# Summing the convolution taps of the first two blocks in PSUM with transposes, and taking the first unit's weights first

## The chip, the cores and the metric

One core of a Trainium2 chip runs the whole program. The metric is the device time of one execution in microseconds, lower is better; a run's number is the median of several executions. Beside it stands one execution taken with the hardware profiler, whose span reaches from its first to its last instruction.

The engines by the names that the profile uses: PE is TensorE's matmul and PEld its weight load, DVE is VectorE, ACT is ScalarE, POOL is GpSimd, and SP is SyncE, which issues all of this kernel's DMAs.

## The reference

Three steps follow each other. x has the shape (2, 4096, 192) and the generated weights (2, 4096, 8, 7).

```python
w = softmax(weight_gen over its last axis)          # 7 taps for each of 8 heads
x_unf = x_pad[:, s + k, :]                          # k = 0..6, six zeros ahead
out[b, s, h, g] = sum_k w[b, s, h, k] * x_unf[b, s, k, h, g]   # 24 channels a head
x = out.reshape(8192, 192)
g = max(0.01 * (x @ w_in), x @ w_in)                # 192 -> 2048
x = g @ w_out                                       # 2048 -> 192
h = x @ w2_in
g = where(h > 0, h, exp(min(h, 0)) - 1)
x = g @ w2_out
```

All of it is fp32.

## The kernel before, in words

**Tiles.** The 8192 tokens are cut into 16 blocks of 512: 128 partitions with 4 consecutive tokens each (BS = 4). A block passes through a convolution, layer 0 and layer 1. Each layer has 2048 hidden channels, worked in 8 units of 256.

**Two parts for every operand.** To keep fp32 exactness at the PE's faster fp32r rate, every activation and every weight is split into a high part, rounded to fp32r, and a low part, the rest. A product takes three matmuls: low by high, high by low, high by high. Activations are split by ACT (the rounded copy) and DVE (the subtraction).

**Weights** (`split`, lines 196 to 259) come from memory as raw 8-byte words. SP loads a piece into a buffer of the ring `raw` (three buffers); ACT takes the fraction (L217) and the exponent part (L221) into a buffer of ring `t` (two); DVE joins bits (L228, L231) and adds (L238); ACT writes the high part (L241), DVE the low one (L246). `split_in` (lines 264 to 269) makes pieces of the in-weights, `part` 0 for input channels 0 to 127 and `part` 1 for the other 64, folded; `split_out` makes pieces of the out-weights. The first unit of layer 0 needs a piece of 256 columns and one of 128.

**Convolution** (`conv_block`, lines 281 to 411). SP loads the block's generated weights (L288, 112 KB) and its x with six tokens ahead (L291, 960 KB). DVE and ACT make the softmax (L298 to L311). Then DVE multiplies tap by tap (L331), the first tap into the tile `a`, the others into `prod`, and adds each `prod` to `a` (L339): 7 multiplies and 6 adds, each 768 elements a partition. ACT copies channels 128 to 191 doubled side by side (`double`, L374). The PE transposes: 16 matmuls with an identity, each 64 partitions by 128 columns onto 64 output columns, 8 from the doubled copy and 8 from `a` (L388), into the PSUM bank that later holds the block's sums of layer 0. ACT and DVE split the result into `yt` or `xt` (`high`, L393, `low`, L396), the input of layer 0.

**Units.** `phases` (line 182) gives the order of blocks and layers. Blocks 0 and 1 of layer 0 run interleaved, one unit of one, one unit of the other, so that a piece of weights lasts for two units; then block 2 of layer 0, blocks 0 and 1 of layer 1, and from there one phase of each layer in turn. The first four units (`LAG = 4`) have only their in-matmuls (`whole`, line 699: six over the whole array, six over halves of its rows, two at a time), from then on a round (`both`, line 712) interleaves one unit's in-matmuls with the out-matmuls of the unit four before. A unit's tile `h` in PSUM (two buffers) is read by ACT (L552, leaky, or L555 and L559 for layer 1), which makes the high part too (L569); DVE makes the low one (L572).

**The order of the work.** Nothing is ordered by the engines: `Plan.order` (lines 78 to 127) simulates the five queues at build time with estimated costs, and the program is issued in the order that it finds. Whenever an engine is free, it takes the ready task with the smallest key among those whose buffers are free in the rings; a unit's matmuls have the key `s`, its number, and a task gives its buffers back when all its users have ended. For a convolution block with due date `due`, multiplies and adds have keys from `due - 0.8` backwards in steps of `2 * PACE`; block 0 is due at -13.5, block 1 at -0.5. Weight pieces have keys around the number of the unit that needs them first, for the first two 0: load at -6, bits at -1.6, low at -0.7. On the chip each engine works its queue in that order and waits on semaphores.

```python
a = plan.add({"q": max(0.45, 1.44 * z)}, key - 6, load, takes=[raw], delay=2.3)
f = plan.add({"a": 0.2 + 0.46 * z}, key - 1.9, fraction, [a], uses=[raw])
b = plan.add({"a": 0.2 + 0.46 * z}, key - 1.9, unbias, [a], [t], [raw])
b = plan.add({"d": 0.29 + 0.8 * z}, key - 1.6, bits, [b], uses=[t, raw])
b = plan.add({"d": 0.15 + 0.53 * z}, key - 1.3, add, [b, f], uses=[raw, t])
```

Of the kernel before, what the change touches and what calls it, by code (L numbers as in the profile page):

```python
# [8 lines left out]
F32 = mybir.dt.float32  # L9
F32R = mybir.dt.float32r  # L10
I32 = mybir.dt.int32
U32 = mybir.dt.uint32
I64 = mybir.dt.int64
AF = mybir.ActivationFunctionType
ALU = mybir.AluOpType
AX = mybir.AxisListType

P = 128
D = 192
DFF = 2048  # L20
H = 8
K = 7
G = D // H
# [3 lines left out]
BS = 4  # L27
NB = SP // BS
N = BS * P
# [8 lines left out]
AHEAD = 1  # L38

PACE = 0.28  # L40


class Task:
# [87 lines left out]
def conv_moe_kernel(ctx: ExitStack, tc: tile.TileContext, x, wg, wi0, wi1, wo, out):  # L131
    nc = tc.nc

    rings = {
        "xs": (2, [P, BS + PAD, D], F32), "ws": (2, [P, BS * H, K], F32),
        "st": (1, [P, BS * H, 3], F32), "a": (1, [P, BS, D], F32), "prod": (1, [P, BS * D], F32),
        "xt": (1, [P, 4, N], F32R), "yt": (2, [P, 4, N], F32R),
        "h": (2, [P, 2, N], F32), "w": (3, [P, 2 * N], F32),
        "gh": (4, [P, 2 * N], F32R), "gl": (4, [P, 2 * N], F32R),
        "c": (1, [P, N], F32), "o": (1, [P, N], F32),  # L140
        "raw": (3, [P, 512], I64), "t": (2, [P, 512], I32),
    }
    const = ctx.enter_context(tc.tile_pool(name="const", bufs=1))
    sb = ctx.enter_context(tc.tile_pool(name="sb", bufs=1))
# [4 lines left out]
    plan = Plan({r: bufs for r, (bufs, _, _) in rings.items()})  # L149
# [3 lines left out]
    def new(slot):  # L153
        bufs, shape, dt = rings[slot.ring]
        if bufs == 1 or slot.ring == "h":

            tiles, n = lasting.setdefault(slot.ring, ([], [0]))
            if len(tiles) < bufs:
                pool = {"h": ps, "st": small}.get(slot.ring, sb)
                tiles.append(pool.tile(shape, dt, name=f"{slot.ring}{len(tiles)}"))  # L160
            slot.tile = tiles[n[0] % bufs]
            n[0] += 1
            return slot.tile
        pool = small if slot.ring == "ws" else sb
        slot.tile = pool.tile(shape, dt, tag=slot.ring, name=slot.ring, bufs=bufs)
        return slot.tile

    ident = const.tile([P, P], F32, name="ident")
    spare = const.tile([P, 1], F32, name="spare")
    win = {}  # L170
# [15 lines left out]
    bank = {p: acc[n % 2] for n, p in enumerate(phases)}  # L186
# [74 lines left out]
    def first(l, u):  # L261
        return min(at[l, i, u] for i in range(2))

    def split_in(l, part, m0, m1):
        c = slice(m0 // 2 * P, m1 // 2 * P) if part else slice(m0 * P, m1 * P)
        lo = [(win[l, part, 1][:, c], slice(None))]
        names = [("in", l, u) for u in range(m0 // 2, m1 // 2)]
        src = (wi0, wi1)[part][l][:, c]
        split(src, win[l, part, 0][:, c], lo, first(l, m0 // 2), names)

    def split_out(l, k0):
        w = wout[l][:, k0 : k0 + 2, :]
# [5 lines left out]
    xts = {}  # L278
    stored = {}

    def conv_block(i, due):

        xs, ws, st, a = Slot("xs"), Slot("ws"), Slot("st"), Slot("a")
# [29 lines left out]
        first = due - 0.8 - 2 * K * PACE  # L313
        lw = plan.add({"q": 0.45}, first - 8, load_w, takes=[ws], delay=2.3)
        lx = plan.add({"q": 2.7}, first - 7.9, load_x, takes=[xs], delay=2.3)
        t = plan.add({"d": 0.68}, first - 3, top, [lw], [st], [ws])
        t = plan.add({"a": 0.3}, first - 2, exp, [t], uses=[ws])
        t = plan.add({"d": 0.75}, first - 1, total, [t], uses=[ws, st])
        t = plan.add({"d": 0.35}, first - 0.5, scale, [t], uses=[ws, st])
        prod = Slot("prod")  # L320
# [18 lines left out]
            nc.vector.tensor_tensor(out=sums(), in0=sums(), in1=prods(), op=ALU.add)  # L339

        y = [t, lx]
        for k in range(K):
            key = due - 0.8 - PACE * 2 * (K - 1 - k)
            takes = [[a], [prod]][k] if k < 2 else []
            uses = [r for r in [xs, ws, a] + [prod] * (k > 0) if r not in takes]
            y = [plan.add({"d": 0.95}, key, lambda k=k: mult(k), y, takes, uses)]
            if k:
                y = [plan.add({"d": 0.95}, key, add, y, uses=[a, prod])]
        last = y

        x_t = Slot("yt" if i < 2 else "xt")
        xts[0, i] = x_t

        place = Slot("h") if i == 2 else None

        def at_place():
            return place.tile if place else bank[0, i]

        def parts(j):

            return at_place()[:, :, j * N // 2 : (j + 1) * N // 2]

        def slot(j):
            return x_t.tile[:, j, :].rearrange("p (a b) -> p a b", a=2)

        twice = Slot("o")

# [19 lines left out]
                        c = (j * BS + s) * 64  # L387
                        nc.tensor.transpose(at_place()[:, half, c : c + 64], src, ident[r, r])  # L388

        def high(j):  # L390
            if not j:
                new(x_t)
            return nc.scalar.activation(slot(2 * j), parts(j), AF.Copy).ins  # L393

        def low(j):
            return nc.vector.tensor_tensor(  # L396
                out=slot(2 * j + 1), in0=parts(j), in1=slot(2 * j).bitcast(F32), op=ALU.subtract
            ).ins

        n = phases.index((0, i))  # L400
        free = stored[phases[n - 2]] if i > 2 else []
        p = [place] if place else []
        t = plan.add({"a": 0.6}, due - 0.2, double, last + free, [twice], [a])
        t = plan.add({"pe": 0.95}, due, transpose, [t], p, [a, twice])

        k = due + (0.3 if i < 3 else 1.35)
        b = plan.add({"a": 0.55}, k, lambda: high(0), [t], [x_t], p)
        c = plan.add({"a": 0.55}, k + 0.1, lambda: high(1), [b], uses=[x_t] + p)
        b = plan.add({"d": 0.66}, k + 0.2, lambda: low(0), [b], uses=[x_t] + p)
        c = plan.add({"d": 0.66}, k + 0.3, lambda: low(1), [c], uses=[x_t] + p)  # L410
        return [b, c]

    def evac(l, i, after, key):
        A, B = (bank[l, i][:, j, :] for j in range(2))
# [240 lines left out]
    low = {}  # L655
# [130 lines left out]
```

## Time and profile before

| | |
|---|---|
| median of 3 runs | 1167.04 us (1166.29 to 1167.16) |
| the profiled execution | 1164.52 us |
| its span | 1162.7 us |
| PE busy | 1119.4 us, 96% |
| DVE busy | 808.2 us, 70% |
| ACT busy | 788.3 us, 68% |
| multiplies of the convolution into `prod` (L331) | 96, 955 ns each |
| its adds (L339) | 96, 955 ns each |

The busy time of an engine is the sum over its instructions; its share is of the span. The matmuls overlap in a pipeline, so a busy PE need not be at its peak. The profile is of one execution, 2.5 us faster than the median of the runs.

### The profile page before, as it was taken

The page shows a single profiled execution, that of the slowest core. Times are in us where ns is not written, and L with a number is a line of the kernel's source. Part 1 is how long each engine was busy: PE and PEld are TensorE (multiplying, and loading weights), DVE is VectorE, ACT ScalarE, POOL GpSimd, SP SyncE. Part 2 cuts the span into 40 slices and gives each one's busy share as a digit, 9 for nine tenths or more (in the row PEclk, how much of TensorE's full clock was granted, in tenths as well). Part 3 has the DMA queues.
Part 4 walks back from the last instruction along what each step waited for, and adds up shares of the span by engine and source line. Part 5 has one row for each costly group of instructions (what it writes and reads, how often), then busy time and mean ns, then how long its engine had stood idle before and what let it go on. Part 6 is the DMA issues. An engine that isn't in the chain of part 4 may idle for free.

```text
span 1162.7 us, 23771 instructions
## 1 busy us (share of the span) xinstructions
PE 1119.4 (96%) x9920; PEld 930.9 (80%) x9920; DVE 808.2 (70%) x1050; ACT 788.3 (68%) x1022; POOL 0.7 (0%) x6
## 2 busy tenths in 40 slices
PE   0699999999999999999999999999999999999998
PEld 0488998888888888888888888888888888888886
DVE  8999998948568494865948578494865839464464
ACT  1687898658586675857658576675857657585675
POOL 0000000000000000000000000000000000000000
PEclk9999999999999999999999999999999999999999
DMA  3424230000101001010100101001010000000000
GB/s 136 147 87 127 76 94 15 19 35 2 52 1 52 2 1 52 1 53 2 52 1 1 53 1 52 1 1 53 1 53 1 15 1 1 15 2 15 1 1 28
DMA packets 12620, 37.97 MB, mean 33 GB/s; under 512 B 1504, under 2 KB 3680, under 8 KB 12512
## 3 DMA queue, kind: packets, MB, share of 16 engines
q1 hardware_dynamic: 12512, 36.44, 9.8%
q8 instruction: 78, 1.28, 0.5%
q14 instruction: 30, 0.25, 0.1%
HBM read 30.15 MB, written 6.29 MB: 31 GB/s over the span
## 4 chain that ended last, share of the span: by engine, by line
PE 96%; DVE 3%; DMA 0%; ACT 0%; issue 0%; ACTq 0%; SPq 0%; DVEq 0%
PE acc L630 50%; PE h L630 45%; DVE prod L331 1%; DVE a L339 1%; PE acc L388 1%; DMA xs<-x_in 0%; ACT w L552 0%; DVE a L331 0%; DVE yt L396 0%; DVE t L231 0%; DVE w L563 0%; ACT yt L393 0%; DVE t L228 0%; DVE yt L440 0%; DVE c L425 0%
## 5 line engine op out<-in xcount | busy, mean ns | idle before, releaser
L630 PE MATMUL acc<-gh,wout 64*128 64x512 f32 (+1 forms) x3048 | 972.7, 386 | 0.0
L630 PE MATMUL acc<-gl,wout 64*128 64x512 f32 (+1 forms) x2032 | 785.5, 387 | 0.0
L630 PE MATMUL h<-yt,win 64*128 64x512 f32 (+1 forms) x2568 | 612.6, 389 | 18.5 <-ACT win L241 14.2
L630 PEld LDWEIGHTS acc<-gh,wout 64*128 64x128 f32 (+1 forms) x3048 | 560.1, 184 | 57.3
L630 PEld LDWEIGHTS h<-yt,win 64*128 64x128 f32 (+1 forms) x2568 | 470.2, 185 | 69.7 <-ACT win L241 14.3
L630 PE MATMUL h<-xt,win 64*128 64x512 f32 x2016 | 476.7, 386 | 0.1
L572 DVE TENSOR_TENSOR gl<-w,gh 128x1024 fp32r<-128x1024 f32 (+1 forms) x257 | 312.2, 1220 | 162.6 <-ACT gh L569 161.9
L630 PEld LDWEIGHTS acc<-gl,wout 64*128 64x128 f32 (+1 forms) x2032 | 374.1, 184 | 38.7 <-issue 0.4
L630 PEld LDWEIGHTS h<-xt,win 64*128 64x128 f32 x2016 | 370.6, 184 | 38.9 <-ACT gh L569 0.5
L569 ACT ACTIVATE gh<-w 128x1024 fp32r<-128x1024 f32 (+1 forms) x257 | 268.0, 1049 | 2.9
L552 ACT ACTIVATE w<-h 128x1024 f32<-128x1024 f32 x128 | 131.5, 1027 | 200.9 <-PE h L630 198.5
L563 DVE SCALAR_TENSOR_TENSOR w<-w,h 128x512 f32<-128x512 f32 x256 | 164.2, 683 | 141.4 <-ACT w L559 141.4
L555 ACT ACTIVATE w<-h 128x1024 f32<-128x1024 f32 x129 | 131.2, 1018 | 121.2 <-PE h L630 120.9
L559 ACT ACTIVATE w<-w 128x512 f32<-128x512 f32 x256 | 147.7, 624 | 3.9
L331 DVE TENSOR_TENSOR prod<-xs,ws 128x768 f32<-128x768 f32 x96 | 91.7, 955 | 1.9
L339 DVE TENSOR_TENSOR a<-a,prod 128x768 f32<-128x768 f32 x96 | 91.7, 955 | 1.5
L425 DVE TENSOR_TENSOR c<-acc,c 128x512 f32<-128x512 f32 (+1 forms) x32 | 22.0, 687 | 32.4 <-ACT o L455 23.6
L388 PE MATMUL acc<-ident,o 64*128 64x64 f32 x120 | 6.5, 231 | 19.6 <-ACT o L374 19.6
L388 PEld LDWEIGHTS acc<-ident,o 64*128 64x128 f32 x120 | 6.4, 147 | 21.6 <-issue 19.8
L418 ACT ACTIVATE c<-acc 64x512 f32<-64x512 f32 x32 | 19.1, 596 | 6.1 <-PE acc L630 5.2
L217 ACT ACTIVATE raw<-raw 128x384 int32<-128x384 uint32 (+3 forms) x30 | 17.2, 572 | 8.0 <-DMA raw<-wi_in 6.1
L231 DVE SCALAR_TENSOR_TENSOR t<-raw,t 128x384 int32<-128x384 int32 (+3 forms) x30 | 17.6, 585 | 1.0
(43 smaller groups left out, 257.8 us busy)
## 6 DMA issues: line engine op xcount, KB each, us to landing
xs<-x_in SPq DMA_DIRECT2D x16, 960.0 KB, 4.9
raw<-wo_in SPq DMA_DIRECT2D x16, 384.0 KB, 3.2
raw<-wi_in SPq DMA_DIRECT2D x10, 512.0 KB, 3.8
out_t<-o SPq DMA_DIRECT2D x16, 256.0 KB, 3.6
out_t<-c SPq DMA_DIRECT2D x16, 128.0 KB, 3.2
ws<-wg_in SPq DMA_DIRECT2D x16, 112.0 KB, 2.1
raw<-wi_in SPq DMA_DIRECT2D x2, 256.0 KB, 6.7
raw<-wi_in SPq DMA_DIRECT2D x1, 384.0 KB, 2.7
```

Of the source, the lines that this page charges most:

```text
L331: nc.vector.tensor_tensor(out=prods() if k else sums(), in0=xs.tile[:, k : BS + k, :].rearrange("p s (h g) -> p (s h) g", g=G), in1=ws.til ...
L339: nc.vector.tensor_tensor(out=sums(), in0=sums(), in1=prods(), op=ALU.add)
L388: nc.tensor.transpose(at_place()[:, half, c : c + 64], src, ident[r, r])
L418: nc.scalar.activation(new(c)[0:64], B[64:P], AF.Copy)
L425: nc.vector.tensor_tensor(out=c.tile[0:n], in0=B[0:n], in1=c.tile[0:n], op=ALU.add)
L552: nc.scalar.activation(cols(w), flat(), AF.Prelu, alpha=0.01)
L555: nc.scalar.activation(cols(w), flat(), AF.Relu, scale=-1.0)
L559: nc.scalar.activation(c, c, AF.Exp, scale=-1.0)
L563: nc.vector.scalar_tensor_tensor(out=c, in0=c, scalar=1.0, in1=h.tile[:, j, :], op0=ALU.subtract, op1=ALU.max,)
L569: nc.scalar.activation(cols(gh), cols(w), AF.Copy)
L572: return nc.vector.tensor_tensor(out=cols(gl), in0=cols(w), in1=cols(gh).bitcast(F32), op=ALU.subtract).ins
L630: i = nc.tensor.matmul(out_ap, w, x_ap, start=start, stop=stop).ins
```

## The change

For blocks 0 and 1 (`ADDED = 2`) the sum over the taps moves. DVE still multiplies each tap, now always into a buffer of `prod`, which has three instead of one. For each tap ACT copies the doubled channels (into a new ring `dup` of two) and the PE transposes product and doubled copy, 16 matmuls in transpose mode, into the block's PSUM bank; the first of tap 0 opens the accumulation and all the others add to it. The sum over seven taps is so formed in PSUM, and the six adds, the tile `a` and the single group of transposes fall away for these two blocks. The other 14 blocks are computed as before.

The two weight pieces of layer 0's first unit get the key `FIRST = -20.15` in place of 0, so load, bits, add and low have keys from -26.15 to -20.85. Ring `t` has three buffers instead of two, and the memory set aside for descriptors of software DMAs is cut to 1024 bytes. The functions `at_place`, `parts`, `slot`, `high` and `low` move up within `conv_block`, and `splits` holds the four tasks that stood at its end.

```diff
+FIRST = -20.15
+
+ADDED = 2
...
-        "st": (1, [P, BS * H, 3], F32), "a": (1, [P, BS, D], F32), "prod": (1, [P, BS * D], F32),
+        "st": (1, [P, BS * H, 3], F32), "a": (1, [P, BS, D], F32), "prod": (3, [P, BS * D], F32),
...
-        "c": (1, [P, N], F32), "o": (1, [P, N], F32),
-        "raw": (3, [P, 512], I64), "t": (2, [P, 512], I32),
+        "dup": (2, [P, N], F32), "c": (1, [P, N], F32), "o": (1, [P, N], F32),
+        "raw": (3, [P, 512], I64), "t": (3, [P, 512], I32),
...
-        split(src, win[l, part, 0][:, c], lo, first(l, m0 // 2), names)
+
+        key = first(l, m0 // 2) if (l, m0) != (0, 0) else FIRST
+        split(src, win[l, part, 0][:, c], lo, key, names)
...
+        def splits(t, k, p):
+            b = plan.add({"a": 0.55}, k, lambda: high(0), [t], [x_t], p)
+            c = plan.add({"a": 0.55}, k + 0.1, lambda: high(1), [b], uses=[x_t] + p)
+            b = plan.add({"d": 0.66}, k + 0.2, lambda: low(0), [b], uses=[x_t] + p)
+            c = plan.add({"d": 0.66}, k + 0.3, lambda: low(1), [c], uses=[x_t] + p)
+            return [b, c]
...
+        if i < ADDED:
+            def product(k, tap):
+                nc.vector.tensor_tensor(
+                    out=new(tap).rearrange("p (a g) -> p a g", g=G),
+                    in0=xs.tile[:, k : BS + k, :].rearrange("p s (h g) -> p (s h) g", g=G),
+                    in1=ws.tile[:, :, k : k + 1].to_broadcast([P, BS * H, G]),
+                    op=ALU.mult,
+                )
+
+            def doubled(tap, dup):
+                v = tap.tile.rearrange("p (s d) -> p s d", d=D)[:, :, P:D]
+                src = v.unsqueeze(2).to_broadcast([P, BS, 2, P // 2])
+                dst = new(dup).rearrange("p (s a b) -> p s a b", s=BS, a=2)
+                nc.scalar.activation(dst, src, AF.Copy)
+
+            def added(k, tap, dup):
+                for j in range(2):
+                    for s in range(BS):
+                        for half in range(2):
+                            r = slice(64 * half, 64 * half + 64)
+                            src = tap.tile[r, s * D : s * D + P]
+                            if j:
+                                src = dup.tile[r, s * P : (s + 1) * P]
+                            c = (j * BS + s) * 64
+                            nc.tensor.matmul(
+                                at_place()[:, half, c : c + 64], src, ident[r, r],
+                                start=k == j == s == 0,
+                                stop=(k, j, s) == (K - 1, 1, BS - 1), is_transpose=True,
+                            )
+
+            t = []
+            for k in range(K):
+                tap, dup = Slot("prod"), Slot("dup")
+                key = due - 0.8 - PACE * 2 * (K - 1 - k)
+                y = [plan.add({"d": 0.95}, key, lambda k=k, b=tap: product(k, b), y, [tap], [xs, ws])]
+                u = plan.add(
+                    {"a": 0.62}, key, lambda b=tap, d=dup: doubled(b, d), y, [dup], [tap]
+                )
+                t = [
+                    plan.add(
+                        {"pe": 1.2}, key, lambda k=k, b=tap, d=dup: added(k, b, d), [u] + t,
+                        uses=[tap, dup],
+                    )
+                ]
+            return splits(t[0], due + 0.3, [])
...
-    nc = bacc.Bacc("TRN2", target_bir_lowering=False, num_devices=1)
+    nc = bacc.Bacc(
+        "TRN2", target_bir_lowering=False, num_devices=1, dynamic_dma_scratch_size=1024
+    )
```

## Rows read from the trace of the kernel before

**Rows 1.** The page, part 1: busy us (share of the span) and instructions.

```profile
PE 1119.4 (96%) x9920; PEld 930.9 (80%) x9920; DVE 808.2 (70%) x1050; ACT 788.3 (68%) x1022; POOL 0.7 (0%) x6
```

**Rows 2.** Waits of PE, whole span: line, awaited, us in total, times, longest.

```profile
PE acc L388 <- ACT o L374: 19.6, 1, 19.6
PE h L630 <- ACT win L241: 14.2, 1, 14.2
PE h L630 <- DVE yt L396: 2.2, 1, 2.2
PE h L630 <- DVE win L246: 1.0, 1, 1.0
```

**Rows 3.** The chain that ended last, in order of time: start us, us, what.

```profile
1.19 4.75 DMA xs<-x_in
...
35.44 0.87 DVE a L339
...
36.70 4.10 PE h L630 x10
...
40.82 1.02 ACT w L552
...
43.60 9.22 PE h L630 x36
...
54.66 0.45 PE acc L630 x4
...
206.05 0.49 PE acc L388 x16
```

**Rows 4.** Timeline: start us, us, engine line op out<-in xcount [idle before, releaser].

```profile
4.20 0.39 DVE L306 TENSOR_REDUCE st<-ws 128x32 f32<-128x224 f32 x1 [0.46 <-ACT ws L302]
...
6.04 0.96 DVE L331 TENSOR_TENSOR a<-xs,ws 128x768 f32<-128x768 f32 x1 [0.42 <-DMA xs<-x_in]
...
9.33 0.44 ACT L217 ACTIVATE raw<-raw 128x256 int32<-128x256 uint32 x1 [5.17 <-DMA raw<-wi_in]
...
19.60 0.69 PE L388 MATMUL acc<-ident,o 64*128 64x64 f32 x8 [19.60 <-ACT o L374]
...
20.05 0.66 PE L388 MATMUL acc<-ident,a 64*128 64x64 f32 x8
...
36.23 0.62 DVE L246 TENSOR_TENSOR win<-t,win 128x256 fp32r<-128x256 f32 x2
...
38.76 0.33 SPq L213 DMA_DIRECT2D raw<-wi_in  x1
...
40.98 0.41 PE L388 MATMUL acc<-ident,a 64*128 64x64 f32 x8
...
50.84 0.68 DVE L246 TENSOR_TENSOR win<-t,win 128x512 fp32r<-128x512 f32 x1
...
52.43 0.39 PE L630 MATMUL acc<-gl,wout 64*128 64x512 f32 x1
```

**Rows 5.** Groups of instructions from 0 to 44 us: busy us, mean ns, idle before.

```profile
L339 DVE TENSOR_TENSOR a<-a,prod 128x768 f32<-128x768 f32 x12 | 11.5, 958 | 0.4
...
L231 DVE SCALAR_TENSOR_TENSOR t<-raw,t 128x256 int32<-128x256 int32 (+2 forms) x4 | 1.7, 426 | 0.1
L238 DVE CUSTOM_DVE_ANT_0 t<-raw,t 128x512 uint16<-128x512 uint16 (+2 forms) x4 | 1.7, 422 | 0.1
...
L374 ACT ACTIVATE o<-a 128x512 f32<-128x512 f32 x2 | 1.3, 630 | 8.6 <-DVE a L339 8.6
...
L228 DVE TENSOR_SCALAR t<-t 128x256 int32<-128x256 int32 (+2 forms) x4 | 1.1, 286 | 0.0
```

**Rows 6.** Stretches: us, busy of PE, PEld, DVE, ACT, POOL, clock, DMA, GB/s; last: PE alone.

```profile
43.60:110.00 66.40, 65.75 (x548) 52.53 (x550) 62.78 (x102) 53.90 (x78) 0.00 (x0) 0.97 0.35 109
110.00:180.00 70.00, 69.48 (x612) 66.50 (x610) 65.93 (x103) 61.96 (x91) 0.00 (x0) 1.00 0.27 79
...
45.50:46.50 1.00, 1.00 (x5) 0.50 0.00 0
```

More of the change, by code (lines that the diff above doesn't have):

```diff
@@ L341, in conv_block, with parts, slot, high @@
         y = [t, lx]
+        x_t = Slot("yt" if i < 2 else "xt")
+        xts[0, i] = x_t
+        def parts(j):
+            return at_place()[:, :, j * N // 2 : (j + 1) * N // 2]
+        def slot(j):
+            return x_t.tile[:, j, :].rearrange("p (a b) -> p a b", a=2)
+        def high(j):
+            if not j:
+                new(x_t)
+            return nc.scalar.activation(slot(2 * j), parts(j), AF.Copy).ins
+        def low(j):
+            return nc.vector.tensor_tensor(
+                out=slot(2 * j + 1), in0=parts(j), in1=slot(2 * j).bitcast(F32), op=ALU.subtract
+            ).ins
@@ new lines, in splits, with at_place @@
+        def splits(t, k, p):
[4 more added lines that the diff above has]
+            return [b, c]
+        def at_place():
+            return place.tile if place else bank[0, i]
+        place = None
+        if i < ADDED:
[40 more added lines that the diff above has]
+            return splits(t[0], due + 0.3, [])
@@ L349, in conv_block @@
         last = y
-        x_t = Slot("yt" if i < 2 else "xt")
-        xts[0, i] = x_t
         place = Slot("h") if i == 2 else None
[L356 to L364, printed above, removed]
         twice = Slot("o")
@@ L388, in transpose @@
                         nc.tensor.transpose(at_place()[:, half, c : c + 64], src, ident[r, r])
[L390 to L398, printed above, removed]
         n = phases.index((0, i))
@@ L406, in conv_block @@
         k = due + (0.3 if i < 3 else 1.35)
[L407 to L411, printed above, removed]
+        return splits(t, k, p)
     def evac(l, i, after, key):
```

## The prediction

> **What bounds the kernel now.** I read four views in this order: the page, the waits of the PE queue, the chain that ended last, and the timeline of the first 45 us. The page gives the PE 96% of the span [rows 1], so only the time in which it stands still, or runs at half clock, can be won without taking matmuls away. The waits say where it stands still: 19.6 us until block 0's doubled copy, 14.2 us until the first piece of first-layer weights, 1.0 until that piece's low part and 2.2 until block 1's split activations [rows 2]. All four lie before 43.6 us. The chain says what filled that time [rows 3]: the load of x until 5.94 us, then VectorE's multiplies and adds from 6.04 on [rows 4], block 1's last add ending at 36.3; then unit 0 on the PE (36.70 to 40.8), its leaky evacuation on ACT, and from 43.60 matmuls almost without a gap. The head is VectorE's: 13 multiplies and adds for each of two blocks at a pitch of 0.99 us (11.5 us of work and 0.4 of idle for twelve) [rows 5]. From 43.6 to 180 us the PE is busy for 135.2 of 136.4 us, while VectorE is busy for 128.7 [rows 6]: it keeps up there with 6% to spare. So what the change is worth is how much earlier unit 1, now at 43.60, can start, less what is given back by 180 us.
>
> **The change, part by part.**
> (a) *Twelve adds go from VectorE.* L339 runs 12 times in the head, 11.5 us of work and 0.4 of idle [rows 5]: 11.9 us off the head's chain. The 14 multiplies stay.
> (b) *Fourteen doublings on ACT instead of two.* 0.63 us each [rows 5], 7.6 us more. ACT waited 8.6 us for VectorE's sums before the two there are now [rows 5], and one doubling (0.63) fits inside a multiply's pitch (0.99). Cost nothing, but for the last one of a block, which stood on the path before as well.
> (c) *Fourteen taps on the PE instead of two groups of transposes, 16 matmuls each.* No row shows transposes that accumulate. The nearest are the plain ones: 1.11 us for 16 at 19.60, 0.82 at 40.57 to 41.39 (the row of its second half is shown), 0.49 at 206 [rows 3, 4]. I take 0.8 to 1.1. Eight of a tap's 16 need only the product, so they run while ACT doubles; the pitch stays VectorE's 0.99. Below 1 us a tap costs nothing until the last of each block; above, each 0.1 us costs 1.4 us over 14 taps.
> (d) *The first unit's two weight pieces (256 and 128 columns) go ahead.* On SP their loads, 256 and 128 KB, pass block 0's x, 960 KB, which took 4.75 us [rows 3]. By size that delays it by at most 384/960 of 4.75, 1.9 us, to 7.8; the pass over VectorE below is later, so this costs nothing. On VectorE, bits (0.29 + 0.43), add (0.42) and low (0.62 for both) [rows 4, 5] of two pieces now stand before block 0's first product, which also waits about 1.0 us for ACT's fraction and unbias (0.44 each [rows 4]). These 2.5 us (the 128-column piece is shorter) and the 1.0, less the 0.9 that VectorE idled there (0.46 and 0.42 [rows 4]), put the first product at 8.7 instead of 6.04. These steps stood in front of unit 0 before too, except the low parts at 36.23 [rows 4]: for the end of block 1 only 0.6 us is new, and the 1.0 of waiting.
> (e) *The order.* The planner, followed by hand with its own costs, rings and keys, charges a tap 1.2 us of PE against 0.95 for a product, so that a product sometimes has no free buffer in its ring of three, and the planner puts other VectorE work there: block 1's softmax, which had to come anyway, and the bits of the next two weight pieces (256 columns, then 384). At 0.71 mean [rows 5], more for the wider, I count 1.7 us.
>
> Sum for VectorE: block 1 ended at 36.3; minus 11.9, plus 0.6, plus 1.0, plus 1.7, is 27.7 us for its last product.
> On the PE the planner lands unit 0 behind block 1's fifth tap, whose product ends at 24.8 (27.7 less two products and the 384-column bits). With a doubling and the second half of a tap that is 26.1. Unit 0 took 4.10 us [rows 3]: 30.2. Queued behind it on the PE are block 1's last two taps, so whoever waits for these waits for unit 0: block 1's splits. From unit 0's end to unit 1 it was 2.8 us (40.82 to 43.60: leaky, two highs, first low [rows 3]); two taps instead of one group add some 0.4. Unit 1 starts at 33.2: **10.4 us earlier**.
> Ends of this: were unit 0 to slip in earlier than the fifth tap, only block 1 counts: 27.7 + 0.1 + 0.63 + 0.55 and the 2.2 us from the transposes' end (41.39 [rows 4]) to 43.60 give 31.2, a gain of 12.4. Were add, low and bits of further pieces (some 2.5 us) also set ahead of the last products, the gain is 7.9.
>
> (f) *After unit 1.* Between 27.7 and block 1's lows VectorE has some 4 us for the add and low steps that it did between 37 and 43 before; I find it about level with before relative to unit 1. Its tightest date is the 512-column piece of unit 4: its load waits on SP for a raw buffer, was issued at 38.76, its low part ended at 51.5, and the round that needs it began at 52.43 [rows 4], 0.9 us of margin. In the new order the load goes out near 28.5, 13 us before need as against 13.7, but without a 960 KB load just ahead of it in the queue. I take no loss. The rings' extra buffers and the smaller DMA scratch are in no wait.
>
> The profiled execution had a span of 1162.7 and a time of 1164.52, 2.5 us under the median of the runs; minus 10.4 it would be 1154.1. Off the median, **1167.04 - 10.4 = 1156.6 us**.
>
> **A rule weighed on the way.** In this trace unit 0's nine array passes (six whole, three in pairs of halves) took 4.10 us, 456 ns each; in the steady part four half-array matmuls, two passes, take 0.45 [rows 3]. So unit 0 ran at the 1.2 GHz level, though the clock column still says 1.00 there; later it does show 0.50, for 45.5 to 46.5 [rows 6], after the PE had stood idle from 41.4 to 43.6. Fourteen taps of transposes now run before unit 0, so it could find the clock raised. The Trainium skill, "TensorE: Matmul & The Clock Gate", Part 4, says that transposes do not count as PE work for the clock. By that rule unit 0 keeps its 4.10; no run here shows it yet.
>
> **Rivals.**
> *The clock is up when unit 0 starts* (0.13). For: the PE is busy with taps most of the time from 10 us on. Against: the single group at 19.60 left no trace of a faster clock 15 us later. Price: half of unit 0's 4.10 and half of the 3.2 us at 0.50 near 45 us: up to 3.7 more gained, about 1153.
> *Given back* (0.20). The head is won, but with VectorE 94% busy between 44 and 180 [rows 6] the moved order leaves some piece late: unit 4's 512-column weights first, whose margin is 0.9, or a block's sums. Each us late is a us of PE idle. At 3 to 8 us of it: 1160 to 1165, 1161.5 in the middle; for 0.05 of the 0.20 the rest is within 0.2%, 2.3 us, about what a measurement can tell here.
> *Slower: the taps set the pace* (0.05). An accumulating transpose may cost more than a plain one, with three products and two doublings in flight only. VectorE then waits for buffers. The tap decides it: up to about 1.0 us it hides, at 0.99 + 10.4/14 = 1.73 us the gain is gone, and at twice the slowest seen (2.2) the 14 taps cost 16.9 against 10.4 gained: 1173.5. Against: the accumulating matmuls of the steady part stream without a gap, and the plain groups stay under 1.11.
> *The sums don't form in PSUM.* Then the output is wrong and the time the same, since nothing waits on values; it adds no case.
>
> **How the numbers follow.** Forecast 0.62, at 1156.6, its own range 1154.6 to 1159.1 from the two ends of the order. Below it the raised clock reaches to 1152, above it the middle of the giving back, with a little for its larger half, to 1162.5; outside stay the far end of the giving back and the slow taps, some 0.15 with a little of the low end. Faster by over 0.2%: 0.62 + 0.13 + 0.15 = 0.90; same 0.05; slower 0.05.
>
> **What would show it.** Right: no add on VectorE before block 2's; the first product near 8.7; block 1's last product near 28; unit 0 near 26 to 30 and unit 1 near 33, with PE idle after it as before (about 1.2 us up to 180). A tap should take 0.5 to 1.1 us. Wrong: products waiting for a PE tap at L331 (slow taps); a new wait of the PE for weights between 40 and 180 (given back); unit 0 done in about 2 us (clock); or weight steps standing between the products for more than 3 us, so that block 1 ends after 31.

## The result, and the profile after

Before: 1166.67 us (median of 4 runs, 1166.29 to 1167.16). After: **1154.87 us** (4 runs, 1154.56 to 1154.98). The ratio is 0.9898 with a 95% interval of 0.9881 to 0.9915: 11.8 us gained where 10.4 were forecast, and 1154.87 lies inside the range of 1152.0 to 1162.5. The profiled executions differ by less, 1164.52 to 1154.56 (spans 1162.7 to 1152.8, 9.9 us): the four runs of before lie between 1166.29 and 1167.16 and its profiled execution, at 1164.52, was shorter than all of them, while after's runs, the profiled one among them, lie within 0.5. The traces therefore have 9.9 us to explain, not 11.8.

The page of the changed kernel, part 1, answers to [rows 1]:

```profile
PE 1130.3 (98%) x10112; PEld 975.7 (85%) x10112; DVE 795.3 (69%) x1038; ACT 795.7 (69%) x1034; POOL 0.7 (0%) x6
```

VectorE has 12 instructions and 12.9 us less, ACT 12 instructions and 7.4 us more, the PE 192 matmuls more (fourteen taps of 16 for two groups of 16).

The waits of PE after (line, awaited, us in total, times, longest) answer to [rows 2]:

```profile
PE acc L405 <- DVE prod L383: 11.2, 2, 10.9
PE h L688 <- DVE yt L364: 2.8, 1, 2.8
PE acc L405 <- ACT dup L394: 2.4, 4, 0.9
PE h L688 <- ACT w L610: 0.7, 1, 0.7
```

A tap is one product with its doubled copy, 16 transposes in all; L383 is the product, L394 its doubling, L405 the tap on the PE, L364 the low part of a block's input, L610 is the leaky step of a unit on ACT, L621 the elu step of a layer 1 unit on VectorE. The two long waits of before, 19.6 for block 0's doubled copy and 14.2 for the first weights, are gone. What is left is one wait of 10.9 until the first product, small ones for doublings, and 2.8 for block 1's splits, where before it was 2.2.

The timeline after (start us, us, engine line op out<-in xcount, idle before and releaser), first the first 36 us, then the PE alone, answers to [rows 4]:

```profile
9.76 2.69 DVE L383 TENSOR_TENSOR prod<-xs,ws 128x768 f32<-128x768 f32 x3 [0.96 <-DMA xs<-x_in]
10.87 0.69 PE L405 MATMUL acc<-ident,prod 64*128 64x64 f32 x8 [10.87 <-DVE prod L383]
...
11.92 0.64 PE L405 MATMUL acc<-ident,prod 64*128 64x64 f32 x8
12.35 0.65 PE L405 MATMUL acc<-ident,dup 64*128 64x64 f32 x8
...
23.66 4.33 PE L688 MATMUL h<-yt,win 128*128 128x512 f32 x12
...
25.95 0.89 DVE L242 CUSTOM_DVE_ANT_0 t<-raw,t 128x512 uint16<-128x512 uint16 x2
...
27.62 0.89 DVE L250 TENSOR_TENSOR win<-t,win 128x256 fp32r<-128x256 f32 x2
28.06 0.42 PE L405 MATMUL acc<-ident,dup 64*128 64x64 f32 x8
28.31 0.42 PE L405 MATMUL acc<-ident,prod 64*128 64x64 f32 x8
28.42 0.96 DVE L383 TENSOR_TENSOR prod<-xs,ws 128x768 f32<-128x768 f32 x1
29.46 1.05 ACT L627 ACTIVATE gh<-w 128x1024 fp32r<-128x1024 f32 x1
30.41 0.62 ACT L394 ACTIVATE dup<-prod 128x512 f32<-128x512 f32 x1
31.08 0.46 PE L405 MATMUL acc<-ident,dup 64*128 64x64 f32 x8 [0.75 <-ACT dup L394]
32.06 0.53 ACT L245 ACTIVATE wout<-t 128x384 fp32r<-128x384 f32 x1
32.47 1.07 ACT L361 ACTIVATE yt<-acc 128x512 fp32r<-128x512 f32 x2
33.58 1.29 DVE L364 TENSOR_TENSOR yt<-acc,yt 128x512 fp32r<-128x512 f32 x2 [0.22 <-ACT yt L361]
34.32 1.97 PE L688 MATMUL h<-yt,win 128*128 128x512 f32 x4 [2.78 <-DVE yt L364]
...
43.19 0.39 PE L688 MATMUL acc<-gl,wout 64*128 64x512 f32 x1
```

Unit 0 (23.66) stands among the taps, not behind the last one. Unit 1 starts at 34.32 for 43.60 before, 9.3 us earlier; the first round with second-layer matmuls at 43.19 for 52.43, 9.2 earlier. The remaining 0.7 us of the 9.9 come after that.

The groups of the first 34 us after (busy us, mean ns, idle before) answer to [rows 5]:

```profile
L383 DVE TENSOR_TENSOR prod<-xs,ws 128x768 f32<-128x768 f32 x14 | 12.8, 948 | 1.2 <-DMA xs<-x_in 1.0 <-PE acc L405 0.2
L394 ACT ACTIVATE dup<-prod 128x512 f32<-128x512 f32 x14 | 8.6, 624 | 6.6 <-DVE prod L383 5.7 <-PE acc L405 0.8
```

No add is left in the head. VectorE idled 0.2 us for a product's buffer to be freed by a tap, ACT 0.8 for a doubling's.

**The stretch that decides.** From the first round to the moment with 920.0 us to go, before and after do the same work: 1684 matmuls in both. By that moment VectorE has done the same instructions too, 341 before and twelve adds fewer, 329, after. Busy time of PE, PEld, DVE, ACT, POOL, then clock and DMA, from the first round to that moment and from the start to it, before:

```profile
52.43:242.70 190.27, 189.10 (x1684) 165.12 (x1682) 171.84 (x264) 153.39 (x217) 0.00 (x0) 1.00 0.24 72
0.00:242.70 242.70, 204.53 (x1762) 175.15 (x1764) 217.80 (x341) 173.03 (x253) 0.70 (x6) 0.99 0.28 88
```

and after:

```profile
43.19:232.80 189.61, 188.85 (x1684) 171.92 (x1682) 169.35 (x257) 152.31 (x213) 0.00 (x0) 1.00 0.22 67
0.00:232.80 232.80, 215.49 (x1954) 192.09 (x1956) 204.92 (x329) 180.76 (x265) 0.70 (x6) 0.99 0.29 92
```

So the 9.9 us are 9.2 from the earlier first round and 0.7 behind it. Behind it the PE stands still for 0.76 us (189.61 less 188.85), where before it was 1.17 (190.27 less 189.10). VectorE's work up to the same moment fell by 12.9 us, from 217.80 to 204.92. In the changed kernel VectorE's chain, with x's load ahead of it and steps of ACT at its end, sets the head; from unit 1 on the PE is the bound, busy for all but 0.76 us. The experiments show what happens when VectorE does not keep up behind the first round.

### The profile page after: what moved, and what is told of

The parts are those of the page before. It is cut to its first block, busy times and chain, and to the rows that moved or that the text cites. A ratio compares the mean times of both kernels' runs of the same rounds, so it can differ in the third digit from the quotient of the medians.

```text
span 1152.8 us, 24185 instructions
## 1 busy us (share of the span) xinstructions
PE 1130.3 (98%) x10112; PEld 975.7 (85%) x10112; DVE 795.3 (69%) x1038; ACT 795.7 (69%) x1034; POOL 0.7 (0%) x6
## 4 chain that ended last, share of the span: by engine, by line
PE 97%; ACT 1%; DMA 1%; SPq 0%; issue 0%; DVE 0%; ACTq 0%
PE acc L688 50%; PE h L688 46%; DMA raw<-wi_in 1%; PE acc L460 1%; PE acc L405 0%; ACT w L610 0%; ACT dup L394 0%; ACT gh L627 0%; ACT raw L221 0%; ACT c L476 0%; ACT yt L361 0%; DVE prod L383 0%; ACT wout L245 0%; SPq L297 0%; SPq L217 0%
## 5 line engine op out<-in xcount | busy, mean ns | idle before, releaser
L610 ACT ACTIVATE w<-h 128x1024 f32<-128x1024 f32 x128 | 131.4, 1027 | 200.1 <-PE h L688 191.3
L621 DVE SCALAR_TENSOR_TENSOR w<-w,h 128x512 f32<-128x512 f32 x256 | 164.3, 684 | 141.3 <-ACT w L617 141.1
L337 DVE TENSOR_TENSOR prod<-xs,ws 128x768 f32<-128x768 f32 x84 | 80.2, 955 | 1.6
L345 DVE TENSOR_TENSOR a<-a,prod 128x768 f32<-128x768 f32 x84 | 80.2, 955 | 1.1
L405 PE MATMUL acc<-ident,prod 64*128 64x64 f32 x112 | 8.2, 289 | 11.2 <-DVE prod L383 11.2
L242 DVE CUSTOM_DVE_ANT_0 t<-raw,t 128x768 uint16<-128x768 uint16 (+3 forms) x30 | 17.2, 581 | 0.5
```

The source lines that it names most:

```text
L337: nc.vector.tensor_tensor(out=prods() if k else sums(), in0=xs.tile[:, k : BS + k, :].rearrange("p s (h g) -> p (s h) g", g=G), in1=ws.til ...
L610: nc.scalar.activation(cols(w), flat(), AF.Prelu, alpha=0.01)
L621: nc.vector.scalar_tensor_tensor(out=c, in0=c, scalar=1.0, in1=h.tile[:, j, :], op0=ALU.subtract, op1=ALU.max,)
```

## The experiments

Each edit is against the changed kernel unless another is named. Times are medians, ratios are against the kernel before on the same chip.

### 1. The sums alone: the first weights not taken first

```diff
-        key = first(l, m0 // 2) if (l, m0) != (0, 0) else FIRST
+        key = first(l, m0 // 2)
```

> The first unit's weights go back to their old keys; the taps stay in PSUM. Theory (unit 1's start sets the time): without the weight steps in front, block 0's first product is back near 6.1 us instead of 9.8, block 1's last product ends near 25.5 instead of 29.4, all its taps stand before unit 0 on the PE, and unit 1 follows unit 0 at once, near 31 instead of 34.3: 1151 to 1152 us, 3 to 4 faster than the changed kernel. Rival (the weights taken first are what made the head short, since the PE waited 14.2 us for them): unit 0 starts near 27 instead of 23.7 and everything after it 3 us later, 1158 us.

Measured: 1157.86 us (1156.71 to 1158.90), ratio 0.9931 (0.9917 to 0.9946), span 1155.4. The waits of PE in it:

```profile
PE h L688 <- DVE w L621: 5.1, 3, 3.4
PE h L688 <- ACT w L610: 1.4, 2, 0.8
```

Its PE in the timeline:

```profile
9.18 0.64 PE L405 MATMUL acc<-ident,prod 64*128 64x64 f32 x8
...
13.27 0.41 PE L405 MATMUL acc<-ident,prod 64*128 64x64 f32 x8
...
21.28 0.63 PE L405 MATMUL acc<-ident,prod 64*128 64x64 f32 x8
...
24.57 9.29 PE L688 MATMUL h<-yt,win 128*128 128x512 f32 x36
...
37.99 0.50 PE L688 MATMUL acc<-gl,wout 64*128 64x512 f32 x1
...
174.40 0.46 PE L688 MATMUL h<-yt,win 64*128 64x512 f32 x1 [3.38 <-DVE w L621]
```

The head came out as the theory said, and better than in the changed kernel: the taps begin at 7.26, units 0 and 1 run on without a gap from 24.57, and the first round begins at 37.99, 5.2 us before that of the changed kernel. Yet the kernel ends 2.6 us of span later than it, so the theory's time was missed; the rival's 1158 was met, but not by its way, since unit 0 starts at 24.57 and not near 27. The gain is given back behind the first round, the greater part of it at 166 and at 174 us, where the PE waits 1.3 and 3.4 us for the elu step at L621 on VectorE:

```profile
37.99:235.40 197.41, 191.59 (x1684) 179.90 (x1686) 173.87 (x269) 154.94 (x219) 0.00 (x0) 0.99 0.23 70
170.00:180.00 10.00, 6.62 (x46) 5.96 (x44) 9.93 (x17) 3.76 (x5) 0.00 (x0) 0.83 0.33 110
```

The same 1684 matmuls take 197.41 us here, 7.8 more than in the changed kernel. PE idle time makes 5.1 of that (5.82 for 0.76); the other 2.7 is PE busy time (191.59 for 188.85). At least a part of the 2.7 is the clock: behind the 3.4 us wait the granted clock falls, to 0.50 between 176 and 178 us. At 170 to 180 VectorE is busy for 9.93 of 10 us, with block 3's multiplies and adds between the weight and elu steps.

### 2. The weights alone, in two ways

First the changed kernel with no block summed on the PE (its rings and its order stay), then the kernel before with nothing but the new key:

```diff
-ADDED = 2
+ADDED = 0
```

```diff
-        split(src, win[l, part, 0][:, c], lo, first(l, m0 // 2), names)
+        key = first(l, m0 // 2) if (l, m0) != (0, 0) else -20.15
+        split(src, win[l, part, 0][:, c], lo, key, names)
```

> The first unit's weights are taken first, but both blocks keep their adds and the single group of transposes. Theory: unit 0 starts early, but block 1's last add ends near 40 us, because 12 adds at 0.99 us are back on VectorE and the weights are ahead of them; unit 1 starts near 44 as in the kernel before, 1166 to 1168 us. Rival (the weights are the gain): the PE's wait of 14.2 us for them is gone and most of the 11.8 us stays won, 1156 to 1159 us.

> The kernel before with nothing changed but the key of the first unit's two weight pieces; rings as before, adds on VectorE. Theory (VectorE's work up to some 190 us sets the time, and the order of block 3's sums decides how much of that time VectorE stands idle; the run with the weights first and the new rings lost 4.7 us there): the head is as before to 1 us, VectorE's work is the same 166 us, and the time is 1165 to 1168 us if block 3's sums come as early as before, 1169 to 1172 if they come late. Rival (the early weights take the PE's wait of 14.2 us away): 1156 to 1160 us.

Measured: the first 1170.48 us (1169.00 to 1171.94), ratio 1.0040 (1.0025 to 1.0055), slower than before; the second 1166.87 (1166.22 to 1167.66), ratio 1.0010 (1.0001 to 1.0019). In both unit 0 moves forward as meant, to 27.4 and 27.1 from 36.70, and unit 1 does not: 43.71 and 43.44 for 43.60. Unit 1 needs block 1, and block 1 is VectorE's. The row of unit 1's start in each:

```profile
43.71 8.94 PE L688 MATMUL h<-yt,win 128*128 128x512 f32 x36 [2.16 <-DVE yt L364]
```

```profile
43.44 10.07 PE L631 MATMUL h<-yt,win 128*128 128x512 f32 x36 [2.14 <-DVE yt L397]
```

So the new key gains nothing by itself; the 11.8 us need the adds gone. The first kernel missed its theory's 1166 to 1168, the second met its own. Against the kernel before on the same chip the first loses 4.1 us and the second 1.3. From the first round to the moment with 920.0 us to go the first takes 195.3 us and the second 192.6; the PE waits 4.8 us for L621 in the first, as in experiment 1, and 1.4 us for the same step in the second. What differs between them is the rings, the DMA scratch and the order that the planner makes of them; which of these it is was not tried.

### 3. One block instead of two

```diff
-ADDED = 2
+ADDED = 1
```

> Only block 0 sums in PSUM; block 1 adds on VectorE again. Theory: six adds are back on the chain, but VectorE no longer has to wait for free product buffers in block 1; block 1's last add ends near 34 us and unit 1 starts near 38, 4 us later than in the changed kernel: 1158 to 1160 us. Rival (each block brings half): 1161 us. Second rival (only block 0's sums delayed the PE, block 1's lie beside unit 0): 1155 us.

Measured: 1164.51 us (1162.03 to 1165.50), ratio 0.9981 (0.9971 to 0.9990). Unit 1 starts at 35.89, 7.7 us earlier than before, and all but 2 us of it is given back; again 4.8 us of waiting for L621. None of the three times expected was met. Half the adds are not half the gain, and once more an early start was not an early end.

### 4. The taps without transpose mode

```diff
-                                stop=(k, j, s) == (K - 1, 1, BS - 1), is_transpose=True,
+                                stop=(k, j, s) == (K - 1, 1, BS - 1),
```

> The taps' matmuls with the identity run as plain fp32 matmuls instead of in transpose mode. Theory (transposes leave the PE's clock at its lower level, plain matmuls raise it): a tap costs more at first, then unit 0 takes near 2 us instead of 4.3, and the total is 1153 to 1156 us. Rival (the clock stays low and the plain matmuls take several passes): a tap takes 1.7 us or more, above the 0.99 us of a product, and the head grows by 5 to 10 us, 1160 to 1165 us.

Measured: 1178.65 us (1178.50 to 1179.38), ratio 1.0112 (1.0095 to 1.0129). Its PE in the timeline:

```profile
10.26 1.97 PE L405 MATMUL acc<-ident,prod 64*128 64x64 f32 x16 [10.26 <-DVE prod L383]
11.99 1.95 PE L405 MATMUL acc<-ident,dup 64*128 64x64 f32 x16
13.70 1.95 PE L405 MATMUL acc<-ident,prod 64*128 64x64 f32 x16
...
42.71 1.95 PE L405 MATMUL acc<-ident,dup 64*128 64x64 f32 x16
44.58 4.50 PE L688 MATMUL h<-yt,win 128*128 128x512 f32 x12
...
50.03 1.05 PE L405 MATMUL acc<-ident,dup 64*128 64x64 f32 x16
```

Each half of a tap (eight pieces, here two records each) now starts 1.71 us after the last, 3.4 us a tap; the PE is solid from 10 to 44 us, and it, not VectorE, sets the head. Of the two expectations above the rival's mechanism came, at twice its tap, and neither time was met. This is the prediction's slow-tap rival at work, with its sign; its size was overdrawn. By the rival's working a tap of 3.41 us costs 14 times 2.42 against 10.4 gained, 23.5 us over before; 12.3 were measured against before on the same chip. The four taps behind unit 0 ran at the raised clock and took 1.8 us each, which is 6.4 of the difference. For the rest it may be that VectorE did in its waits what else stands in its head; that was not shown. Without transpose mode a tap takes over three times VectorE's pitch of 0.99 us.

### 5. Experiment 1 with block 3 hurried

Against experiment 1's kernel:

```diff
-    hurry = {0: 12, 3: 3}
+    hurry = {0: 12, 3: 6}
```

> Taps in PSUM, the first unit's weights at their old keys, and block 3's convolution due three units earlier, so that its sums stand where VectorE idled near 100 to 130 us. Theory (the run with the weights at their old keys won 5 us more in the head and gave them back near 165 to 190 us, because block 3's multiplies and adds stood between the second layer's elementwise steps there): the wait of the PE for L621, 5.1 us, falls to under 1.5, and the time is 1152 to 1154 us. Rival (VectorE has too much work up to 190 us whatever its order): the PE waits as long, at another place, 1156 to 1159 us.

Measured: 1156.20 us (1154.76 to 1157.83), ratio 0.9916 (0.9901 to 0.9931), span 1156.1. The waits of PE in it:

```profile
PE h L688 <- ACT w L610: 4.1, 2, 3.4
PE h L688 <- DVE w L621: 3.6, 3, 2.1
```

The time is the rival's. Block 3's first multiply moved from 128.6 to 116.4 us, and the wait for L621 shrank, from 5.1 us to 3.6, but did not go. The longer wait for L610 is not behind block 3's sums: 3.4 us of it lie in the head, at 35.55, where unit 0 ran at the raised clock (2.54 us) and the first round came at 39.86. So block 3's place in the order is at most a part of the cause. Either VectorE has too much to do by 170 us, or other pieces of its order are late in turn. Experiment 6 takes the work away.

### 6. Experiment 1 without the sums of blocks 2 and 3

Against experiment 1's kernel:

```diff
-            if k:
+            if k and i > 3:
```

> The run with the weights at their old keys, without the 12 adds of blocks 2 and 3: only the last tap's product or the first one is kept, so the sums of these two blocks are left out. Theory (VectorE is the bound up to some 175 us once the head is shorter): its work up to there falls by 11.5 us from 154, the PE's waits for L621 (5.1 us) vanish, and the time is 1149 to 1151 us. Rival (ACT or the buffers of h hold the PE there): the waits stay above 3 us, 1155 to 1158 us.

Measured: 1149.84 us (1149.35 to 1149.97), ratio 0.9864 (0.9847 to 0.9880), span 1148.1. The waits of PE in it that remain behind the head:

```profile
PE h L688 <- ACT w L610: 1.2, 2, 0.6
PE h L688 <- DVE win L250: 0.8, 1, 0.8
```

With the same head (first round at 38.11) the wait for L621 is gone, and 7.3 us of span with it. From the first round to the moment with 920.0 us to go, to be read beside experiment 1's row above:

```profile
38.11:228.10 189.99, 189.26 (x1682) 174.79 (x1684) 163.09 (x257) 154.33 (x219) 0.00 (x0) 1.00 0.24 73
```

It takes 189.99 us instead of 197.41, 7.4 less: 5.1 of PE idle time (0.73 for 5.82) and 2.3 of PE busy time (189.26 for 191.59), which the waits had cost besides. VectorE's work from the start to that moment fell by more, by 10.8 us (194.44 for 205.22). So VectorE's lateness is what gave experiment 1's gain back, and once it is gone the PE is the bound again and the rest of the 10.8 us buys nothing. In the changed kernel, where the PE idles for 0.76 us over the same work, no such wait is left to win.

### 7. A raised clock, forced

Two whole-array plain matmuls of the identity after each tap, and 8 after the last, into an h tile that nobody reads; with more PE work than needed:

```diff
+                warm(8 if (i, k) == (1, K - 1) else 2)
```

> The changed kernel with two more matmuls after each tap (identity by identity, plain fp32, whole array, into a PSUM tile that nothing has written yet), eight after the last one; the output is the same. Theory (the clock is low at unit 0 because transposes don't raise it, and these matmuls do): unit 0 takes near 2.1 us instead of 4.3, the stretch at half clock after 34.8 us is gone, 1152 to 1154 us. Rival (they don't raise it, as the plain taps didn't): a tap grows by some 0.9 us, the products wait for it, and the time is 1157 to 1162 us.

Measured: 1154.83 us (1152.88 to 1155.07), ratio 0.9899 (0.9883 to 0.9916): the time of the changed kernel. From 17.5 us on the taps run at the 2.4 GHz pace, unit 0 takes 2.53 us instead of 4.33 and the stretch at half clock near 36 us is gone. But unit 0 starts at 26.40 instead of 23.66, unit 1 at 35.30 instead of 34.32, and the first round at 43.02 instead of 43.19. Neither of the two times expected was met. The clock was worth little here, with the matmuls that raised it in the way.

### 8. The rings

First one buffer less in t, then with that one more in each of prod and dup. The last was run a second time, together with the changed kernel as it is:

```diff
-        "raw": (3, [P, 512], I64), "t": (3, [P, 512], I32),
+        "raw": (3, [P, 512], I64), "t": (2, [P, 512], I32),
```

```diff
-        "st": (1, [P, BS * H, 3], F32), "a": (1, [P, BS, D], F32), "prod": (3, [P, BS * D], F32),
+        "st": (1, [P, BS * H, 3], F32), "a": (1, [P, BS, D], F32), "prod": (4, [P, BS * D], F32),
-        "dup": (2, [P, N], F32), "c": (1, [P, N], F32), "o": (1, [P, N], F32),
+        "dup": (3, [P, N], F32), "c": (1, [P, N], F32), "o": (1, [P, N], F32),
```

> The changed kernel with two buffers of ring t instead of three. Theory (the third buffer only lets the planner take weight steps earlier): the head is the same to 0.5 us, and the time is within 1.5 us of the changed kernel's, 1154 to 1157 us. Rival (the third buffer keeps the weights of the stretch near 100 to 180 us in time): PE waits of 3 us or more appear there, 1158 us or more.

> The changed kernel with four product and three doubling buffers (and two buffers of ring t again, for room). Theory (block 1's last product waited in the planner's order for a buffer held by a tap behind unit 0, with 2.4 us of weight steps put ahead of it): the products run without a gap and end near 27 us instead of 29.4, all taps stand before unit 0, unit 1 follows it near 32 instead of 34.3; 1152 to 1154 us unless block 3's sums come late again. Rival (doublings and evacuations on ACT set the end of the head): unit 1 stays near 34, 1155 us.

> The kernel with four product and three doubling buffers and two of ring t once more, beside the changed kernel on the same chip. Theory (block 1's products no longer wait behind unit 0): 1151 to 1153 us, 2 to 3.5 us under the changed kernel. Rival (the difference came from the chip or the clock): within 1 us of it.

> The changed kernel itself, for the comparison on one chip: 1154 to 1156 us by either theory, 10 to 12 us under the kernel before.

Measured: with t at 2 alone 1155.26 us (1154.92 to 1155.59), ratio 0.9907 (0.9893 to 0.9922): the third buffer does nothing that shows. With prod at 4 and dup at 3 as well, 1151.90 (1150.96 to 1152.95), ratio 0.9879 (0.9864 to 0.9893). Again, on one chip: 1152.39 (1151.51 to 1153.24) against 1154.62 (1154.51 to 1154.66) for the changed kernel. **The larger rings win another 2.2 us**, the runs of the two do not overlap, and this is the fastest complete version. Which of prod and dup does it was not tried apart. Its PE in the timeline (the second time), then its row from the first round on:

```profile
14.06 0.64 PE L405 MATMUL acc<-ident,prod 64*128 64x64 f32 x8
...
15.80 0.42 PE L405 MATMUL acc<-ident,prod 64*128 64x64 f32 x8
...
20.25 0.69 PE L405 MATMUL acc<-ident,dup 64*128 64x64 f32 x8
...
27.16 2.55 PE L688 MATMUL h<-yt,win 128*128 128x512 f32 x12
30.60 5.02 PE L688 MATMUL h<-yt,win 128*128 128x512 f32 x24 [0.90 <-DVE yt L364]
...
40.19 0.50 PE L688 MATMUL acc<-gl,wout 64*128 64x512 f32 x1
```

```profile
40.19:230.00 189.81, 189.06 (x1682) 165.23 (x1684) 171.47 (x264) 153.68 (x217) 0.00 (x0) 1.00 0.24 73
```

All fourteen taps now stand ahead of unit 0, which starts 3.5 us later than in the changed kernel, while unit 1 starts 3.7 us earlier (30.60). The first round comes 3.0 us earlier, at 40.19 for 43.19, and behind it the two kernels take the same: 189.81 and 189.61 us to the same moment, with the same VectorE work up to it (204.97 and 204.92 us). Units 0 to 3 also ran faster here, 10.1 us for 13.4, at the raised clock. An estimate from these rows says that this was worth little: at the changed kernel's 13.4 us they would end near 40.5, 0.3 after the first round's start, since the PE stands 1.8 us there for a weight step on VectorE.

**The variants in one table.** The span is the first round's start, the time from there to the moment with 920.0 us to go (1684 matmuls in each, to within two), and these 920.0 us. The last column is VectorE's work from the start to that moment.

| kernel | first round | from there on | PE idle in it | PE busy in it | VectorE busy |
|---|---|---|---|---|---|
| before | 52.4 | 190.3 | 1.2 | 189.1 | 217.8 |
| weights alone, in the kernel before | 53.4 | 192.6 | 2.6 | 190.0 | 218.0 |
| weights alone, in the changed kernel | 52.5 | 195.3 | 5.5 | 189.8 | 217.9 |
| one block | 45.6 | 196.6 | 5.5 | 191.1 | 211.3 |
| sums alone | 38.0 | 197.4 | 5.8 | 191.6 | 205.2 |
| sums alone, block 3 hurried | 39.9 | 196.2 | 4.4 | 191.8 | 204.8 |
| sums alone, no adds in blocks 2 and 3 | 38.1 | 190.0 | 0.7 | 189.3 | 194.4 |
| changed | 43.2 | 189.6 | 0.8 | 188.9 | 204.9 |
| larger rings | 40.2 | 189.8 | 0.8 | 189.1 | 205.0 |

The first round alone does not order the times. Where VectorE keeps up behind it, the rest takes 189.6 to 190.3 us whatever the head was; where the PE waits for L621 for over 1 us in all, it takes 2 to 8 us more. The amount of VectorE's work does not tell the two cases apart: the sums alone, the changed kernel and the larger rings have the same 205 us. The key for the first weights does not pay by an earlier unit 0 (experiment 2) and not in the head, which it makes 5.2 us longer. With it VectorE keeps up behind the first round, which is worth 7.8, and the difference is its 2.6 us.

## Why the prediction was right, and where it was not

**The forecast held**, at 1156.6 for 1154.87; in the profiled executions 9.9 us for 10.4. The mechanism held too: VectorE's shorter head lets unit 1 start 9.3 us earlier, and nothing is given back. That 9.3 and 10.4 lie so near is in part luck. The path was not that of the main sum, over unit 0, but that of the upper end (12.4), and late terms of 1.7 and 1.5 us, in (e) and (b) below, took it back to 9.3. The main sum has a slip besides: 30.2 + 2.8 + 0.4 is 33.4 for unit 1 and not 33.2, a gain of 10.2. Point by point:

(a) *Twelve adds off VectorE, 11.9 us.* Shown: twelve instructions and 12.9 us less work up to the same moment, and experiment 2 shows that nothing is gained with the adds in place.

(b) *Doublings at no cost.* The duration was right (0.624 for 0.63), the cover was not complete, so this term was not nothing. The last doubling stood ready at 29.38, when its product ended, and began at 30.41, behind unit 0's gh step (29.46, 1.05 us). Block 1's highs then began at 32.47, 0.93 after the last tap's end at 31.54, with a wout step and what goes before it on ACT in front of them. Against the bare chain of the prediction's upper end this makes 1.5 us: 4.94 from the last product's end to unit 1, for 0.1 + 0.63 + 0.55 + 2.2 = 3.48.

(c) *Taps of 0.8 to 1.1 us.* Right: halves follow at 0.43 us at the 1.2 GHz pace (0.87 a tap) and at 0.25 (0.5) after unit 0. A product waited 0.2 us in all for a tap.

(d) *The first product at 8.7.* **This term was undersized**: 9.76. VectorE was through with the weight steps and the softmax by 8.8; then it idled 0.96 us for x's load, which the prediction had put at 7.8 at the latest by a share of the bytes and called covered. Two loads of 384 KB in all ahead of it cost x some 3.8 us (5.94 to about 9.7), not 1.9; 0.9 of it is that x's own load was issued at 2.11 instead of 1.19.

(e) *The order.* Unit 0 slipped in two taps earlier than forecast, behind block 1's third, and so left the path, as the upper end had it. But that end's 12.4 us did not come. The last product ended at 29.38 for 27.7: 1.06 from (d), and the other 0.6 is put down to more weight steps than the 1.7 counted. They stood there because the product had no free buffer: its slot was held by a tap queued behind unit 0, and from 26.0 to 28.42 VectorE did weight steps instead. Unit 1 at 34.32 is the sum: 31.2 (upper end) + 1.7 + 1.5 = 34.4. The larger rings of experiment 8 remove this cause: their last product ends at 26.0 and unit 1 moves to 30.6 (their unit 0 also ran at the raised clock).

(f) *Level after unit 1.* It held for this kernel, with 0.76 us of PE idle behind the first round for 1.17 before, and the first round to the end shorter by 0.7. But this was less safe than the prediction had it: from the first round to the end the changed kernel takes 1109.6 us, experiment 1 takes 1117.4 and experiment 3 1116.6.

**The rivals.** *Given back* did not happen here and did in experiments 1, 3 and 5, with the mechanism as told (VectorE late, the PE waiting) but on another wait: the elu step around 170 us, with block 3's sums between, and not unit 4's weights. Of the two things that this rival named, weights and a block's sums, it is the second. *Slow taps* needed a dearer tap, and experiment 4 made one. *The clock up at unit 0* did not come in the profiled executions of the changed kernel (4.33, and 4.07 the second time, for 4.10 before), and experiment 7 shows that it would have been worth little unless it came free. The prediction's rule, the earlier start less what is given back, holds in every row of the table. Its main weakness is that (f) followed VectorE to one date only, unit 4's weights, and so had no row from which to tell when it falls behind later.

**Left open.** Why VectorE falls behind with the sums alone and not with the larger rings, whose first round is only 2.2 us later and whose VectorE work up to the same moment is the same. It lies in the planner's order or in the time left to VectorE; moving one block (experiment 5) did not settle it.

## What to carry to other kernels

When two engines are both some 90% busy or more for a long stretch, an earlier start of one is kept only as far as the other keeps up. Find a point from which on the work is the same in both kernels, check that by the counts of instructions, and compare the time up to it and the time behind it apart; in the second, look for waits on the other engine. Such a wait can cost more than its length: in experiment 1, 5.1 us more of idle PE came with 2.7 us more of busy PE. A reduction over taps whose results go through a TensorE transpose anyway can be summed there at half a microsecond a tap at the raised clock and 0.87 at the lower one, provided that it stays in transpose mode; the rings between the engines should be deep enough for a unit of other work to stand in the queue. Loads moved ahead of another on the same queue delayed it here by twice their share of the bytes; look at what waits for the load first.

## What the runs showed of the hardware

*Transposes that accumulate cost what plain ones do.* A tap in the steady clock took 0.5 us, as the plain group did ([rows 3], 0.49). Out of transpose mode, the same pieces took 1.71 us per eight instead of 0.43, 4.0 times as long (experiment 4). The Trainium skill, "TensorE: Matmul & The Clock Gate", Terms, says that transpose mode is four times faster for fp32; the trace agrees.

*Taps alone can raise the clock, and not always.* In experiment 1 eight pieces took 0.64 us until 10 us, 0.41 at 13.3 and 0.63 to 0.69 again at 21, with nothing but taps on the PE; the granted clock reads 0.57 for 20 to 30 us there, unit 0's start included. In experiment 8's larger rings the pace rose near 15.5 us, fell by 19.5 and rose again before unit 0, which took 2.55 us instead of 4.33. In the changed kernel, with the same taps, it did not rise until unit 0 had run in the first profiled execution. In the second the taps took 0.46 us from 20.41 on, and the clock fell again while unit 0 ran (0.50 for 25 to 27 us; 4.07 us). The rule weighed in the prediction, from the Trainium skill, "TensorE: Matmul & The Clock Gate", Part 4, that transposes do not count as PE work for the clock, does not hold in these traces; unit 0 kept its time in the changed kernel all the same.

*A busy PE need not raise it.* In experiment 4 the PE ran plain fp32 pieces of 64 by 64 without a gap from 10 to 44 us at the 1.2 GHz pace (1.95 us a group from first to last, 1.05 after unit 0). What unit 0's whole-array matmuls have that these lack was not settled.

*The clock column starts at 1.00.* It reads 1.00 for that whole stretch, as it does over unit 0 at 4.10 and 4.33. In these traces, before the column's first change the pace of the matmuls tells the level, and the column does not.
